# One-bank PSUM tiles and a five-block state scan in a decay-attention and mixer kernel

## The chip, the cores and the metric

The kernel runs on one core of a Trainium2 chip. The metric is the device time of one execution in microseconds (us). The engines are named as in the profile: PE (TensorE, matrix products; PEld are its weight loads), DVE (VectorE), ACT (ScalarE), POOL (GpSimd) and SP (SyncE, which issues DMAs). Each engine works off its own instructions in the order written; semaphores tie the engines together. SBUF is the working memory; PSUM, in banks of 512 fp32 columns on 128 partitions, takes the results of PE.

## What is computed

Decay attention over four batches and eight heads (768 positions, head width 64, blocks of 64 positions), and behind it a mixer with two products over the positions and two over the channels. Cut to what matters:

```python
# attention, for each batch b and head h; lam[h] is the decay
for b in range(nb):                         # nb = 12 blocks of 64
    intra = einsum('bhic,bhjc->bhij', qb, kb) * Dmask     # lam ** (i - j), i >= j
    intra = einsum('bhij,bhjd->bhid', intra, vb)
    inter = einsum('bhid,bhde->bhie', qb * lam_pow, kv_state)
    out[block b] = intra + inter
    kv_state = lam ** 64 * kv_state + einsum('bhsd,bhse->bhde', kb * rev_pow, vb)
# mixer, on x = out as (4, 768, 512)
u = x + (maximum(x.T @ w_tok1, 0) @ w_tok2).T
return u + maximum(u @ w_ch1, 0) @ w_ch2
```

## The kernel before

Two heads at a time form a pair; there are 16 pairs (4 batches, 4 pairs each). A chunk is 128 positions, two blocks `y` = 0 and 1 on partitions 0 to 63 and 64 to 127; a pair has `NC` = 6 chunks. The order of all engines is the order of the source (`manual_schedule`), so a loop written by hand (L717) sets who stands behind whom.

In pass `i` of this loop, with `j = i - 1`, PE does in turn: `scores(i+1)`, whose results DVE multiplies by the mask in `weigh`; `state(i+1)`; `carry(i, False)`; `carry(j, True)`; `outputs(j)`; the transposes of `turn_k(i+2)` and, for the first eight pairs, `turn_q_rows`; then groups of work of the token mixing (`token_hidden`, `token_out`), between which `turn_back(j, 0)` and `turn_back(j, 1)` stand. Calls of `later` put pieces of the weights' conversion (L455 to L470, L623, L651) on ACT, DVE and POOL in between.

`state` (L298) makes for each chunk the two sums over its blocks, `kv[0]` and `kv[1]`, each in a bank of its own (`k0`, `k1`), 44 matmuls of 64 by 64 a pair (L309). A chunk's sum of both blocks is made in SBUF, in `both`: ACT scales `kv[0]` by the decay of a block (L314), DVE adds `kv[1]` (L315). `both` has six places per state element, the first of them zero, so that the scan L317 over `D` × 6 elements begins each row of states anew (`keep` holds the decay, and zero at each first place). L325 makes the states of the odd blocks. POOL then copies the half of the states that is needed on the other partitions to `st` (L333, `place`), since `carry` (L381) multiplies heads crosswise.

`xTs[i]` collects the transposed output of a pair. It is one tile of two banks, `[P, 2, 512]` (L371), half `y` for the blocks `y`; tags `x0` and `x1` alternate by pair. `carry` and `outputs` (L397) add into it, and ACT copies it to `uT` after chunk 2 and after chunk 5 (L407), each time three chunks of both halves. `turn_back(j, x)` (L414) transposes three chunks back into half `x` of the same tile (L426), and ACT and DVE split the result into `xhi` (L432) and `xlo` (L433). The last group of work of a pass may borrow half 0 (`parting`, L760; `group_bank`, L526); other groups take that one of the banks `s0`, `s1`, `k0`, `k1` which was taken longest ago (`lease`).

Behind attention, two tiles of two banks each give the four entries of `spread` (L811). `bank("sh", ...)` (L115) takes entries 0, 1, 2 in turn, `bank("xT", ...)` entry 3. The products of the mixer's second layer go there: `mm2` (L1112), added to `uT` by L1125, and later `half` (L1167), added by L1182 and L1184. The first layer (`product`, L911) uses `s0` to `k1`.

```python
L371  xTs[i] = ps.tile([P, 2, CB], F32, tag=f"x{i % 2}", bufs=1, name=f"xT{i}")
L760  parting.append(xTs[j][:, 0])
L812  t = ps.tile([P, 2, CB], F32, tag=f"x{x}", bufs=1, name=f"spread{x}")
L813  spread.extend((t[:, 0], t[:, 1]))
```

Of the kernel before, what the change touches and what calls it, by code (L numbers as in the profile page):

```python
# [25 lines left out]
def kernel(  # L26
# [23 lines left out]
    nc = tc.nc  # L50
# [58 lines left out]
    turn_of = {}  # L109
    spread = []  # L110

# [3 lines left out]
    def bank(tag, nm, n):  # L115
        x = turn_of[tag] = turn_of.get(tag, -1) + 1
        if tag == "sc":
            return psum(("s0", "s1", "k0", "k1")[x % 4], nm, n)
        return spread[3 if tag == "xT" else x % 3][:, :n]

# [82 lines left out]

    keep = ap.tile([P, NP, D, NC], F32, name="keep")
    diag = ap.tile([P, D], F32, name="diag")
# [21 lines left out]
    def rows_of(x):  # L227
        return slice(x * D, (x + 1) * D)

    both = ap.tile([P, D, NC], F32, name="both")  # L230
    nc.gpsimd.memset(both, 0.0)
    nc.gpsimd.memset(keep, 0.0)
# [14 lines left out]
    for p in range(NP):  # L247
        nc.gpsimd.tensor_copy(out=keep[:, p, :, 1:], in_=fall2[:, p : p + 1, None].broadcast_to([P, D, NC - 1]))

# [48 lines left out]
    def state(i):  # L298

        b, p = pairs[i]  # L300
        kv = [lease(f"kv{i}{y}", S // 2, f"k{y}").rearrange("p (c e) -> p e c", e=D) for y in range(2)]
        for c in range(NC):
            x, m = spot(i, c)
            for y in range(2):
                if 2 * c + y == 2 * NC - 1:
                    continue
                r = rows_of(y)
                for h in range(2):
                    nc.tensor.matmul(  # L309
                        out=kv[y][rows_of(h), :, c], lhsT=kds[i][r, h, m, x], rhs=vns[i][r, h, c], start=True, stop=True  # L310
                    )
        by = fall[:, p : p + 1]
        n = NC - 1
        nc.scalar.mul(both[:, :, 1:], kv[0][:, :, :n], by)  # L314
        nc.vector.tensor_add(out=both[:, :, 1:], in0=both[:, :, 1:], in1=kv[1][:, :, :n])  # L315
        sv = ap.tile([P, 2, D, NC], F32, tag="sv", bufs=2, name=f"sv{i}")
        nc.vector.tensor_tensor_scan(  # L317
            out=sv[:, 0].rearrange("p e c -> p (e c)"),
            data0=keep[:, p].rearrange("p e c -> p (e c)"),
            data1=both.rearrange("p e c -> p (e c)"),  # L320
            initial=0.0,
            op0=ALU.mult,
            op1=ALU.add,
        )
        nc.vector.scalar_tensor_tensor(  # L325
            out=sv[:, 1], in0=sv[:, 0], scalar=by, in1=kv[0], op0=ALU.mult, op1=ALU.add
        )
        st = ap.tile([P, 2, 3, D], F32, tag="st", bufs=2, name=f"st{i}")
        states[i] = sv, st

        def place():
            for h in range(2):
                nc.gpsimd.tensor_copy(  # L333
                    out=st[rows_of(1 - h)], in_=sv[rows_of(h), :, :, chunks(i, 1 - h)].rearrange("p y e c -> p y c e")
                )

        return place
# [30 lines left out]
    def carry(i, same):  # L368

        if not same:  # L370
            xTs[i] = ps.tile([P, 2, CB], F32, tag=f"x{i % 2}", bufs=1, name=f"xT{i}")  # L371
        sv, st = states[i]
        for m in range(3):
            for x in range(2):
# [5 lines left out]
                for h in range(2):  # L380
                    nc.tensor.matmul(  # L381
                        out=xTs[i][rows_of(h), y, c * D : (c + 1) * D],
                        lhsT=sv[r, y, :, c] if h == x else st[r, y, m],
                        rhs=qss[i][r, h, m, y * D : (y + 1) * D],
                        start=not same and m == 0,
                        stop=False,
                        skip_group_check=True,
                    )

    def outputs(i):  # L390
        b, p = pairs[i]
        for c in range(NC):
            x, m = spot(i, c)
            for y in range(2):
                r = rows_of(y)
                for h in range(2):
                    nc.tensor.matmul(  # L397
                        out=xTs[i][rows_of(h), y, c * D : (c + 1) * D],
                        lhsT=vns[i][r, h, c],
                        rhs=weights_of[i, x][r, h, m],  # L400
                        start=False,
                        stop=(c % 3 == 2),
                        skip_group_check=True,
                    )
            if c % 3 == 2:
                cs = slice(c - 2, c + 1)
                nc.scalar.copy(  # L407
                    out=uT[b][:, p].rearrange("p (c y s) -> p c y s", y=2, s=D)[:, cs],
                    in_=xTs[i][:, :, : S // 2].rearrange("p y (c s) -> p c y s", s=D)[:, cs],
                )  # L410

    x_of = {}

    def turn_back(i, x):  # L414
# [7 lines left out]
        xhi, xlo = x_of[b, half]  # L422
        xp = xTs[i][:, x, : 3 * P]
        cs = slice(3 * x, 3 * x + 3)
# [101 lines left out]
    def group_bank(nm, n):  # L526
        if spread:
            return bank("sh", nm, n)
# [188 lines left out]
    for i in range(-2, NI + 1):  # L717
# [39 lines left out]
        for n in range(3):  # L757
            for f in work[cuts[n] : cuts[n + 1]]:
                if f is work[-1] and n == 2 and len(work) > 1:
                    parting.append(xTs[j][:, 0])  # L760
                f()
# [48 lines left out]
    later(99)  # L810
    for x in range(2):  # L811
        t = ps.tile([P, 2, CB], F32, tag=f"x{x}", bufs=1, name=f"spread{x}")  # L812
        spread.extend((t[:, 0], t[:, 1]))  # L813
    att.close()
# [757 lines left out]
```

## Time and profile before

| | |
|---|---|
| median of 3 runs | 647.53 us |
| lowest and highest | 644.53 and 647.7 us |
| the profiled execution | 649.42 us |
| its span, first to last instruction | 647.6 us |
| busy in the span: PE, DVE, ACT, POOL | 556.8, 403.7, 259.4, 295.9 us |
| mean granted clock of PE | 0.962 |

The span is what the profile shows; 1.8 us lie around it. Busy time is the time in which an engine had an instruction of its own under way, and PE's includes matmuls that overlap. The granted clock is a share of PE's full speed. A wait is named by the instruction that waited and the instruction whose end released it.

### The profile page before, as it was taken

The numbers are of one execution on the slowest core, as the hardware profiler recorded it, in microseconds if no ns is written. First come the engines' busy times: TensorE is split into PE (matmuls) and PEld (weight loads), VectorE is DVE, ScalarE is ACT, GpSimd is POOL, SyncE is SP. The second block draws the span as 40 slices with busy tenths as digits, with TensorE's granted clock in tenths as the row PEclk, the third lists the DMA queues.
The fourth block names the chain that finished last, engine by engine and source line by source line (L and its number), as shares of the span: only waits on it lengthen the run. The fifth ranks groups of instructions, "written<-read, shape, count | busy, mean of one in ns | idle before, by whom it ended". The sixth has DMA issues, their size and how long they took to land.

```text
span 647.6 us, 12886 instructions
## 1 busy us (share of the span) xinstructions
PE 556.8 (86%) x5246; PEld 466.0 (72%) x5246; DVE 403.7 (62%) x589; ACT 259.4 (40%) x471; POOL 295.9 (46%) x257
## 2 busy tenths in 40 slices
PE   5646777867788777989889999999898899999997
PEld 4546776757677676867678778887677678878885
DVE  4446746666657436656777957667946766556555
ACT  3445543354432323445445453434345523323211
POOL 5634543755332504365465685246467721315000
PEclk9987988999989968989999999999999999999999
DMA  9986085466741001657486567895824578656106
GB/s 192 221 201 148 10 175 134 94 151 165 197 96 59 2 1 67 233 222 284 155 303 245 221 254 181 216 333 182 310 74 149 179 174 216 260 211 211 33 1 130
DMA packets 162954, 108.32 MB, mean 167 GB/s; under 512 B 132560, under 2 KB 147408, under 8 KB 162896
## 3 DMA queue, kind: packets, MB, share of 16 engines
q1 hardware_dynamic: 153168, 86.92, 48.6%
q10 hardware_dynamic: 9728, 20.58, 8.5%
q8 instruction: 41, 0.67, 0.4%
q14 instruction: 17, 0.14, 0.1%
HBM read 75.50 MB, written 31.98 MB: 166 GB/s over the span
## 4 chain that ended last, share of the span: by engine, by line
PE 70%; DVE 11%; ACT 8%; DMA 4%; issue 4%; POOL 2%; SPq 0%; ACTq 0%; DVEq 0%; POOLq 0%
PE spread L1167 14%; PE b L911 13%; PE spread L1112 11%; PE d L911 6%; PE a L911 3%; PE xT L381 3%; PE xT L547 3%; DMA raw<-in_moe_w_ch_dram 2%; PE xT L397 2%; PE pu L568 2%; PE ph L547 2%; PE kv L309 2%; PE sc L348 2%; DVE xlo L433 2%; PE xT L426 1%
## 5 line engine op out<-in xcount | busy, mean ns | idle before, releaser
L292 POOL TENSOR_TENSOR qs<-qT,lamp 128x384 f32<-128x384 f32 x32 | 39.2, 1246 | 74.8 <-PE xT L381 74.8
L1125 DVE TENSOR_TENSOR uT<-spread,uT 128x512 f32<-128x512 f32 x63 | 43.3, 687 | 24.8 <-PE spread L1112 24.3
L1112 PE MATMUL spread<-hh,c2h 128*128 128x512 f32 x96 | 39.0, 407 | 9.7 <-DVE uT L1125 9.7
L1112 PE MATMUL spread<-hh,c2l 128*128 128x512 f32 x96 | 38.3, 399 | 0.0
L1112 PE MATMUL spread<-hl,c2h 128*128 128x512 f32 x96 | 38.1, 397 | 0.0
L1182 DVE TENSOR_TENSOR uT<-spread,uT 128x512 f32<-128x512 f32 x50 | 32.8, 684 | 6.2 <-PE spread L1167 6.2
L433 DVE TENSOR_TENSOR xlo<-xT,xhi 128x384 fp32r<-128x384 f32 x32 | 17.8, 556 | 27.9 <-ACT xhi L432 27.5
L397 PE MATMUL xT<-a,vn 64*64 64x64 f32 x720 | 23.2, 232 | 12.8 <-ACT uT L407 8.5
L426 PE MATMUL xT<-ident,uT 128*128 128x128 f32 x96 | 17.9, 300 | 17.9 <-DVE xlo L433 16.7
L333 POOL COPY st<-sv 64x384 f32<-64x384 f32 x32 | 29.0, 907 | 9.4 <-DVE sv L325 8.0
L1112 PEld LDWEIGHTS spread<-hh,c2h 128*128 128x128 f32 x96 | 18.2, 189 | 17.4 <-DVE uT L1125 13.5
L932 POOL TENSOR_TENSOR hl1x<-t,hh1x 128x512 fp32r<-128x512 f32 x8 | 10.6, 1326 | 42.9 <-ACT hh1x L926 42.9
L407 ACT COPY uT<-xT 128x384 f32<-128x384 f32 x32 | 15.3, 479 | 36.9 <-PE xT L397 36.9
L397 PEld LDWEIGHTS xT<-a,vn 64*64 64x64 f32 x720 | 18.9, 138 | 15.2 <-ACT uT L407 10.6
L381 PE MATMUL xT<-qs,sv 64*64 64x64 f32 x352 | 26.2, 284 | 1.1 <-DVE hl L552 1.0
L426 PEld LDWEIGHTS xT<-ident,uT 128*128 128x128 f32 x96 | 12.2, 152 | 20.5 <-DVE xlo L433 18.6
L317 DVE TENSOR_TENSOR_SCAN sv<-keep,both 128x384 f32<-128x384 f32 x16 | 24.0, 1499 | 4.5 <-PE xT L381 3.8
L911 PE MATMUL b<-o,c1h 128*128 128x512 f32 x72 | 26.2, 404 | 0.0
L911 PE MATMUL a<-o,c1h 128*128 128x512 f32 x72 | 25.4, 393 | 0.0
L932 POOL TENSOR_TENSOR tt<-t,tt 128x512 fp32r<-128x512 f32 x12 | 17.0, 1421 | 16.8 <-ACT tt L926 16.8
L381 PEld LDWEIGHTS xT<-qs,sv 64*64 64x64 f32 x352 | 23.7, 205 | 1.4 <-POOL o L684 1.2
L432 ACT CAST xhi<-xT 128x384 fp32r<-128x384 f32 x32 | 15.4, 480 | 22.4 <-PE xT L426 22.4
(423 smaller groups left out, 1842.7 us busy)
## 6 DMA issues: line engine op xcount, KB each, us to landing
c1h<-k SPq DMA_DIRECT2D x12, 896.0 KB, 5.4
c1l<-k SPq DMA_DIRECT2D x12, 896.0 KB, 7.9
raw<-in_moe_w_ch_dram SPq DMA_DIRECT2D x7, 1024.0 KB, 6.6
vn<-in_v_dram SPq DMA_DIRECT2D x15, 384.0 KB, 5.0
k<-c1h ACTq DMA_DIRECT2D x6, 896.0 KB, 4.9
k<-c1l ACTq DMA_DIRECT2D x6, 896.0 KB, 4.0
out_dram<-y SPq DMA_DIRECT2D x72, 64.0 KB, 2.5
c2lx<-k SPq DMA_DIRECT2D x7, 512.0 KB, 4.5
```

Of the source, the lines that this page charges most:

```text
L292: nc.gpsimd.tensor_mul(out=qss[i][:, h].rearrange("p m (y i) -> p (m y) i", i=D), in0=qTs[i].rearrange("p (h n i) -> p h n i", h=2, i=D)[: ...
L333: nc.gpsimd.tensor_copy(out=st[rows_of(1 - h)], in_=sv[rows_of(h), :, :, chunks(i, 1 - h)].rearrange("p y e c -> p y c e"))
L381: nc.tensor.matmul(out=xTs[i][rows_of(h), y, c * D : (c + 1) * D], lhsT=sv[r, y, :, c] if h == x else st[r, y, m], rhs=qss[i][r, h, m, y * ...
L397: nc.tensor.matmul(out=xTs[i][rows_of(h), y, c * D : (c + 1) * D], lhsT=vns[i][r, h, c], rhs=weights_of[i, x][r, h, m], start=False, stop= ...
L426: nc.tensor.transpose(out=xp[:, m * P : (m + 1) * P], in_=uT[b][:, p, c * P : (c + 1) * P], identity=ident)
L433: nc.vector.tensor_sub(out=lo, in0=src, in1=hi.bitcast(F32))
L547: nc.tensor.matmul(out=ph, lhsT=w[:, c, fs], rhs=x[:, c], start=(i == 0), stop=(i == 3 * NC - 1))
L911: nc.tensor.matmul(out=c[into], lhsT=w[:, WI[o], ct], rhs=x[:, ct], start=(first and i == 0), stop=(i == 5), skip_group_check=True,)
L1112: nc.tensor.matmul(out=po, lhsT=w[:, jj, cs], rhs=h, start=(i == 0), stop=(i == 3 * JG - 1), skip_group_check=n >= NG)
L1125: nc.vector.tensor_add(out=ub, in0=two(po), in1=ub)
L1167: nc.tensor.matmul(out=G[into, t], lhsT=w2[:, v, j, t * P : (t + 1) * P], rhs=x, start=(o in (5, 1, 2) and not second and i == 0), stop=(i ...
L1182: nc.vector.tensor_add(out=ub, in0=two(G[into, t]), in1=ub)
```

## The change

Every PSUM tile becomes one bank. `xTs[i]` is a list of two tiles, tags `x00`, `x01`, `x10` and `x11`; `bank` hands out these four tags in the same turn as the entries of `spread`, each time as a new tile. `outputs` copies to `uT` only after chunk 5, once for each bank. `kv[0]` and `kv[1]` are laid out with the chunk innermost, six and five places per state element, so that a matmul writes with a step of 6 or 5 elements. ACT scales `kv[0]` into `half_kv` in SBUF, DVE adds it onto `kv[1]` in PSUM, and the scan reads that sum, over `D` × 5 elements. The first block state, which was the scan's sixth place, is copied from `kv[0]` by two small ACT copies, to `s1` and to `st`; `carry` reads `s1` and `sv[..., c - 1]`, and `place` copies one column less for the even half.

```diff
     def bank(tag, nm, n):
         x = turn_of[tag] = turn_of.get(tag, -1) + 1
         if tag == "sc":
             return psum(("s0", "s1", "k0", "k1")[x % 4], nm, n)
-        return spread[3 if tag == "xT" else x % 3][:, :n]
+        return psum("x11" if tag == "xT" else ("x00", "x01", "x10")[x % 3], nm, n)
...
-    keep = ap.tile([P, NP, D, NC], F32, name="keep")
+    keep = ap.tile([P, NP, D, NC - 1], F32, name="keep")
...
-    both = ap.tile([P, D, NC], F32, name="both")
-    nc.gpsimd.memset(both, 0.0)
+    half_kv = ap.tile([P, D, NC - 1], F32, name="half_kv")
...
-        kv = [lease(f"kv{i}{y}", S // 2, f"k{y}").rearrange("p (c e) -> p e c", e=D) for y in range(2)]
+        kv = [lease(f"kv{i}{y}", D * n, f"k{y}").rearrange("p (e c) -> p e c", c=n) for y, n in enumerate((NC, NC - 1))]
...
-        n = NC - 1
-        nc.scalar.mul(both[:, :, 1:], kv[0][:, :, :n], by)
-        nc.vector.tensor_add(out=both[:, :, 1:], in0=both[:, :, 1:], in1=kv[1][:, :, :n])
-        sv = ap.tile([P, 2, D, NC], F32, tag="sv", bufs=2, name=f"sv{i}")
+        sv = ap.tile([P, 2, D, NC - 1], F32, tag="sv", bufs=2, name=f"sv{i}")
+        st = ap.tile([P, 2, 3, D], F32, tag="st", bufs=2, name=f"st{i}")
+        s1 = ap.tile([P, D], F32, tag="s1", bufs=2, name=f"s1{i}")
+        states[i] = sv, st, s1
+        nc.scalar.mul(half_kv, kv[0][:, :, : NC - 1], by)
+        for h in range(2):
+            nc.scalar.copy(out=(st[rows_of(0), 1, 0] if h else s1[rows_of(0)]), in_=kv[0][rows_of(h), :, 0])
+        nc.vector.tensor_add(out=kv[1], in0=half_kv, in1=kv[1])
         nc.vector.tensor_tensor_scan(
             out=sv[:, 0].rearrange("p e c -> p (e c)"),
             data0=keep[:, p].rearrange("p e c -> p (e c)"),
-            data1=both.rearrange("p e c -> p (e c)"),
+            data1=kv[1].rearrange("p e c -> p (e c)"),
...
         nc.vector.scalar_tensor_tensor(
-            out=sv[:, 1], in0=sv[:, 0], scalar=by, in1=kv[0], op0=ALU.mult, op1=ALU.add
+            out=sv[:, 1], in0=sv[:, 0], scalar=by, in1=kv[0][:, :, 1:], op0=ALU.mult, op1=ALU.add
         )
...
         def place():
             for h in range(2):
+                x = 1 - h
+                cs = range(NC)[chunks(i, x)][1 - x :]
                 nc.gpsimd.tensor_copy(
-                    out=st[rows_of(1 - h)], in_=sv[rows_of(h), :, :, chunks(i, 1 - h)].rearrange("p y e c -> p y c e")
+                    out=st[rows_of(x), :, 1 - x :],
+                    in_=sv[rows_of(h), :, :, cs[0] - 1 : cs[-1] : cs[1] - cs[0]].rearrange("p y e c -> p y c e"),
                 )
...
-            xTs[i] = ps.tile([P, 2, CB], F32, tag=f"x{i % 2}", bufs=1, name=f"xT{i}")
-        sv, st = states[i]
+            xTs[i] = [psum(f"x{i % 2}{y}", f"xT{i}{y}", CB) for y in range(2)]
+        sv, st, s1 = states[i]
...
-                        lhsT=sv[r, y, :, c] if h == x else st[r, y, m],
+                        lhsT=st[r, y, m] if h != x else sv[r, y, :, c - 1] if c else s1[r],
...
-                        stop=(c % 3 == 2),
+                        stop=(c == NC - 1),
                         skip_group_check=True,
                     )
-            if c % 3 == 2:
-                cs = slice(c - 2, c + 1)
-                nc.scalar.copy(
-                    out=uT[b][:, p].rearrange("p (c y s) -> p c y s", y=2, s=D)[:, cs],
-                    in_=xTs[i][:, :, : S // 2].rearrange("p y (c s) -> p c y s", s=D)[:, cs],
-                )
+        for y in range(2):
+            nc.scalar.copy(
+                out=uT[b][:, p].rearrange("p (c y s) -> p y c s", y=2, s=D)[:, y],
+                in_=xTs[i][y][:, : S // 2].rearrange("p (c s) -> p c s", s=D),
+            )
...
-                    parting.append(xTs[j][:, 0])
+                    parting.append(xTs[j][0])
...
-    for x in range(2):
-        t = ps.tile([P, 2, CB], F32, tag=f"x{x}", bufs=1, name=f"spread{x}")
-        spread.extend((t[:, 0], t[:, 1]))
+    mixing = True
```

## Rows read from the trace of the kernel before

**Rows 1.** Busy times by stretches: us, each engine's busy us (instructions), clock, DMA.

```profile
0.00:240.00 240.00, 174.95 (x3585) 157.22 (x3586) 134.23 (x213) 98.62 (x195) 110.07 (x115) 0.92 0.55 125
...
sum 648.00, PE 556.76 PEld 466.04 DVE 403.70 ACT 259.42 POOL 295.92; mean PE 139.19 PEld 116.51 DVE 100.92 ACT 64.86 POOL 73.98
```

**Rows 2.** Tile `xT`, instructions of PE: idle until (us, times).

```profile
  DVE xlo L433: 34.7, 17
  ACT uT L407: 10.3, 18
```

**Rows 3.** Tile `spread`, instructions of PE: idle until (us, times).

```profile
  DVE uT L1125: 9.7, 8
  DVE uT L1184: 5.5, 3
  DVE uT L573: 3.6, 2
  DVE hl L552: 1.8, 1
```

**Rows 4.** Timeline at 121 us: start, us, instruction, [idle before <-releaser].

```profile
121.53 0.56 DVE L433 TENSOR_TENSOR xlo<-xT,xhi 128x384 fp32r<-128x384 f32 x1 [0.28 <-ACT xhi L432]
122.14 0.39 PE L547 MATMUL xT<-xhi,w1h 128*128 128x256 f32 x1 [1.16 <-DVE xlo L433]
```

**Rows 5.** Timeline at 327 us, in the mixer.

```profile
327.20 0.67 DVE L1125 TENSOR_TENSOR uT<-spread,uT 128x512 f32<-128x512 f32 x1
...
327.93 0.50 PE L1112 MATMUL spread<-hh,c2h 128*128 128x512 f32 x1 [1.63 <-DVE uT L1125]
```

**Rows 6.** Timeline at 61 to 65 us, in pass 2.

```profile
61.48 0.90 PE L426 MATMUL xT<-ident,uT 128*128 128x128 f32 x3 [3.51 <-DVE xlo L433]
62.15 0.69 DVE L462 SCALAR_TENSOR_TENSOR uT<-uT 128x512 uint32<-128x512 uint32 x1
...
64.73 0.36 PE L381 MATMUL xT<-qs,st 64*64 64x64 f32 x1
```

**Rows 7.** The page's costliest groups: busy us, mean ns | idle before, releaser.

```profile
L407 ACT COPY uT<-xT 128x384 f32<-128x384 f32 x32 | 15.3, 479 | 36.9 <-PE xT L397 36.9
```

**Rows 8.** Line 317 by itself: ns min/median/max, first and last start.

```profile
L317 DVE TENSOR_TENSOR_SCAN sv<-keep,both x16: 957/1724/1798, 13.1 to 212.2; 128x384 f32<-128x384 f32 x16
```

**Rows 9.** Timelines at 13 and at 54 us, DVE and POOL.

```profile
13.13 0.96 DVE L317 TENSOR_TENSOR_SCAN sv<-keep,both 128x384 f32<-128x384 f32 x1
...
54.24 2.60 POOL L292 TENSOR_TENSOR qs<-qT,lamp 128x384 f32<-128x384 f32 x2 [4.56 <-PE xT L381]
54.25 1.79 DVE L317 TENSOR_TENSOR_SCAN sv<-keep,both 128x384 f32<-128x384 f32 x1 [0.27 <-PE xT L381]
```

**Rows 10.** Line 325 by itself, and who waited for it (us, times).

```profile
L325 DVE SCALAR_TENSOR_TENSOR sv<-sv,fall,kv x16: 612/615/616, 14.2 to 214.0; 128x384 f32<-128x384 f32 x16
...
  PE pu L568: 1.9, 3
  PE ph L547: 1.7, 2
```

**Rows 11.** Line 951, an add whose output `d` is in PSUM: ns min/median/max.

```profile
L951 DVE TENSOR_TENSOR d<-d,u x6: 687/690/700, 269.6 to 383.0; 128x512 f32<-128x512 f32 x6
```

**Rows 12.** Weight loads of line 381: ns min/median/max.

```profile
L381 PEld LDWEIGHTS xT<-qs,sv x352: 183/206/223, 19.1 to 232.8; 64*64 64x64 f32 x176
L381 PEld LDWEIGHTS xT<-qs,st x352: 129/133/228, 19.2 to 232.8; 64*64 64x64 f32 x176
```

**Rows 13.** Stretches from one `state` to `carry`, and from `carry` to `outputs`.

```profile
183.44:184.04 0.60, 0.60 (x56) 0.60 (x49) 0.60 (x2) 0.00 (x0) 0.00 (x0) 1.00 0.00 0
184.04:185.07 1.03, 1.03 (x56) 1.03 (x49) 1.03 (x2) 0.53 (x1) 0.00 (x0) 1.00 0.08 16
```

**Rows 14.** Stretches of 18 matmuls of L547 after a wait, and of 20 without.

```profile
178.85:182.69 3.84, 3.84 (x18) 3.71 (x18) 0.55 (x1) 0.00 (x0) 0.00 (x0) 0.56 0.67 108
173.27:175.43 2.16, 2.16 (x20) 2.16 (x20) 0.73 (x2) 2.15 (x4) 2.04 (x3) 1.00 1.13 342
```

More of the change, by code (lines that the diff above doesn't have):

```diff
@@ L109 @@
     turn_of = {}
-    spread = []
+    mixing = False
     def psum(tag, nm, n):
@@ L247 @@
     for p in range(NP):
-        nc.gpsimd.tensor_copy(out=keep[:, p, :, 1:], in_=fall2[:, p : p + 1, None].broadcast_to([P, D, NC - 1]))
+        nc.gpsimd.tensor_copy(out=keep[:, p, :, 1:], in_=fall2[:, p : p + 1, None].broadcast_to([P, D, NC - 2]))
     kTs, qTs, qss, kds, weights_of, scored = {}, {}, {}, {}, {}, {}
@@ L325, in state @@
         nc.vector.scalar_tensor_tensor(
-            out=sv[:, 1], in0=sv[:, 0], scalar=by, in1=kv[0], op0=ALU.mult, op1=ALU.add
+            out=sv[:, 1], in0=sv[:, 0], scalar=by, in1=kv[0][:, :, 1:], op0=ALU.mult, op1=ALU.add
         )
-        st = ap.tile([P, 2, 3, D], F32, tag="st", bufs=2, name=f"st{i}")
-        states[i] = sv, st
         def place():
             for h in range(2):
+                x = 1 - h
+                cs = range(NC)[chunks(i, x)][1 - x :]
                 nc.gpsimd.tensor_copy(
-                    out=st[rows_of(1 - h)], in_=sv[rows_of(h), :, :, chunks(i, 1 - h)].rearrange("p y e c -> p y c e")
+                    out=st[rows_of(x), :, 1 - x :],
+                    in_=sv[rows_of(h), :, :, cs[0] - 1 : cs[-1] : cs[1] - cs[0]].rearrange("p y e c -> p y c e"),
                 )
@@ L381, in carry @@
                     nc.tensor.matmul(
-                        out=xTs[i][rows_of(h), y, c * D : (c + 1) * D],
-                        lhsT=sv[r, y, :, c] if h == x else st[r, y, m],
+                        out=xTs[i][y][rows_of(h), c * D : (c + 1) * D],
+                        lhsT=st[r, y, m] if h != x else sv[r, y, :, c - 1] if c else s1[r],
                         rhs=qss[i][r, h, m, y * D : (y + 1) * D],
@@ L397, in outputs @@
                     nc.tensor.matmul(
-                        out=xTs[i][rows_of(h), y, c * D : (c + 1) * D],
+                        out=xTs[i][y][rows_of(h), c * D : (c + 1) * D],
                         lhsT=vns[i][r, h, c],
@@ L422, in turn_back @@
         xhi, xlo = x_of[b, half]
-        xp = xTs[i][:, x, : 3 * P]
+        xp = xTs[i][x][:, : 3 * P]
         cs = slice(3 * x, 3 * x + 3)
@@ L526, in group_bank @@
     def group_bank(nm, n):
-        if spread:
+        if mixing:
             return bank("sh", nm, n)
```

## The prediction

> **What bounds the kernel now.** I read first the table of busy times by stretches: TensorE (PE) is busy for 556.8 of 647.6 us, DVE for 403.7, the other engines for less than half. Up to 240 us (attention, with the token mixing woven in) PE is busy for 175.0 of 240 us, at a granted clock of 0.92 [rows 1]. So time can be won where PE stands still. Then I ask for PE's instructions that write the two-bank tiles and what ended PE's idle time before them: for `xT` 34.7 us in 17 waits for L433 and 10.3 us for L407 [rows 2], for `spread` 9.7, 5.5, 3.6 and 1.8 us [rows 3]. That is 65.6 of the 90.8 us in which PE is idle.
>
> Whether these waits are needed is read from the timeline. At 122.14 the first matmul of the group of work that borrows `xTs[j][:, 0]` (`parting`, L760) starts 1.16 us late, behind the L433 of 121.53 [rows 4]. That L433 belongs to `turn_back(j, 1)` and reads the other half. In the mixer the matmul at 327.93 starts 1.63 us late, behind the L1125 of 327.20, which adds the product made just before [rows 5]; yet the halves are taken in turn, and its own was last used three products earlier. So the wait is for the neighbour in the tile. The waits for L407 are another kind: `outputs` writes both halves while the first copy reads from both.
>
> **Part 1, one bank per tile.** The bare chain from the last L426 over one L432 and one L433 is the 1.16 us at 122.14. What is longer is a queue. Pair 1 is an example: PE waits 3.51 us at 61.48, since ACT has three operations of a weight conversion in front of L432. After the change PE goes on at once, but DVE still has L459 and L462 ahead of the second L433. I walk it with this order: L462 ends at 62.15 + 0.69 = 62.84 [rows 6], L433 takes 0.56 [rows 4], so at 63.4 the tile is free that `carry(i+1)` writes. `carry` started at 64.73 [rows 6]; 1.3 of the 3.5 us come through. So of each of the 17 waits I count 1.16 us and nothing of the excess: 19.7 us. Next late is `carry` on L433, behind the conversions. A bare wait comes through whole, because `scores` and `state` (0.6 us and more each) stand between `turn_back` and `carry`.
>
> The copies of `outputs` move behind all 24 + 24 matmuls, one for each bank. 16 waits of 0.57 us go (9.1 of the 10.3 us); in exchange both copies (479 ns each, [rows 7]) now follow the last matmul, and the transposes of `turn_back(j, 0)` need both, because `uT` is ordered by chunks. Where `turn_k`'s six transposes stand between, some 0.2 us are left over; in the last two pairs nothing stands between. I count 14 × 0.4 = 5.6 us.
>
> Behind attention 14 waits, 20.6 us [rows 3]. After the change each bank waits only for its own reader, three products back, which in the cases I looked at was done. But DVE stays as late as it was, and up to 310 us it is late because the conversions wait for loads. I keep two thirds, 13.7 us. This share is a choice; ends 6 and 20.6.
>
> **Part 2, the scan.** L317 takes 957 ns at least and 1724 at the median [rows 8]. At 13.13 it ran alone in 0.96 us; at 54.25 it started with POOL's first L292 and took 1.79 [rows 9]. L325, whose second input is in PSUM, lies in part under the same POOL pair and keeps to 612 to 616 ns in all 16 [rows 10]. So the length comes from two inputs in SBUF beside POOL, and a scan that reads `kv[1]` from PSUM should lose it. For five blocks in place of six I take 957 × 5/6 = 0.80 us, and 0.51 for L325: 0.7 to 0.9 us less a pair where POOL was beside it. This counts where PE waits for L325, which frees the bank of the next group: 3.6 us in five waits [rows 10]. PE comes there up to 0.57 us earlier by part 1, so I count 2.5 us. The add L315 now writes PSUM: adds that do so take 690 ns for 512 columns [rows 11], L433 writes SBUF in 0.56 us for 384 [rows 4], about in proportion, so no cost.
>
> **Part 3, what is added.** Two ACT copies of 64 columns a pair, each between 0.08 (a sixth of L407's 479 ns, for a sixth of its columns) and 0.48 us. They stand between L314 and the first L407; ACT is idle there for 36.9 us in 32 cases, waiting for `outputs` [rows 7], and that hides them. Without this cover they would cost 2.5 to 15 us. L325, two DVE operations later, is the only other one behind them. POOL's second L333 shrinks by a third; POOL is not on the path. `carry` still loads `sv` with a step.
>
> The doubtful edit: L309's 704 matmuls (44 a pair) now write with a step of 6 or 5 elements, where every output of before is contiguous. No row shows such a write. Lower end zero: 44 of them take 0.60 us (183.44 to 184.04, [rows 13]), on four quadrants 55 ns for 64 columns each, 0.85 ns a column, and a slower write can hide behind that. A gain has no reason. The nearest rows are loads with a step: L381's weight load takes 206 ns from `sv` (a step of 6) and 133 from `st` (contiguous) [rows 12], and `carry`'s 44 matmuls, 22 of them with such a load, need 1.03 us [rows 13]: (1.03 − 0.60) / 22 = 20 ns of PE time each. Upper end by this: 704 × 20 = 14 us. I take zero, because a stepped load stands in front of its matmul while a write drains behind it, and keep 14 us for the range.
>
> The Trainium skill speaks against this edit: its page "PSUM — Partial Sum Buffer", section Specifications (TRN2), states lines of 8 bytes and that any non-contiguous access pattern slows matmuls significantly. It gives no figure, and no run of before shows it on an output. By that rule the time would lie at 618 or beyond, where the sum by rows says 604.
>
> **The clock.** From 178.85, behind a wait of 3.1 us, 18 matmuls took 3.84 us at a granted clock of 0.56, near the lower level (1.2 GHz); as many and two more took 2.16 us at 1.00, the level of 2.4 GHz [rows 14]. Such a stretch costs 1.7 us. The long waits become shorter, not nothing, so I count one and a bit: 2 us; ends 0 and 12.
>
> **Sum.** 19.7 + 5.6 + 13.7 + 2.5 + 2 = 43.5 us. The profiled execution took 649.42 us (its span 647.6 and 1.8 around it), 0.3% above the median of 647.53; the same 43.5 us off the median give **604 us**.
>
> **The rivals.**
> - *Everything comes through:* 34.7 + 8 + 20.6 + 3.6 + 6 of clock = 73, so 575 us. Against it: the walk at 61.48. Chance 0.06.
> - *The order on ACT and DVE takes the place of the banks:* conversions stay in front of L432, L433 and L1125, and PE meets the same lateness one step later. Half of 43.5 is kept: 626 us. For it: DVE is busy for 62% of the span [rows 1] and stands in strict order. Against it: the 1.16 us have no queue in them. Chance 0.17.
> - *The step of the output costs 20 ns a matmul:* 604 + 14 = 618 us. Chance 0.10. This is the page's rule at its mild end.
> - *The change doesn't do what it says:* the semaphores still tie neighbours together, and only copy and scan gain, 8 us: 640 us. Against it: rows 4 and 5. Chance 0.05.
> - *Slower:* each matmul of L309 pays the whole 73 ns (206 − 133) of the load's row, and the quadrants don't overlap it: 704 × 73 = 51 us, so 655. It decides from 66 ns a matmul on, (43.5 + 3.2) / 704. The page's rule would be its reason. Against it: the 20 ns of `carry`. Chance 0.06.
>
> **How the numbers follow.** The forecast has 0.56 and reaches from 590 to 618. Low 586 cuts off the first rival; high 632 takes in the stepped one and most of the queue, and leaves out the last two: about 0.82 inside. This kernel can be told from no change by about 0.5%, 3.2 us. Faster by more 0.90, within 0.04 (parts of the fourth rival and of the tails), slower 0.06.
>
> **What would show it.** Right: before instructions that write the `x` banks PE's idle time for L433 and L407 falls from 45 to under 10 us, behind attention from 20.6 to under 7; a new wait of `carry`, on L433 or on the readers of the borrowed bank, has some 10 us; all 16 scans take 0.8 to 0.9 us; 44 matmuls of L309 still take 0.6 us. Wrong: L309 needs over 1 us; the scan from PSUM takes over 1.2 us; `turn_back(j, 0)` waits for L407 in every pair; or the mixer is no shorter, and DVE's lateness was paid at another place.

## The result and the profile after

The changed kernel takes 583.05 us (median; 581.66 to 583.34) where the kernel before, timed beside it, takes 647.62 us: a ratio of 0.9005, 95% interval 0.8971 to 0.904. The gain is 64.6 us; the forecast was 43.5 us, and 583 lies below the range that began at 586.

Where the time went is read from the table of busy times by stretches. I cut both runs at the same places of the program: the first matmul of `product` (L911 before, L912 after), which comes 18 times in groups of 42; the same after 6 and after 12 of these groups; and the end. The columns are those of [rows 1]. First the kernel before, then the one after:

```profile
0.00:237.80 237.80, 172.75 (x3581) 155.44 (x3581) 132.91 (x210) 98.14 (x194) 110.07 (x115) 0.93 0.56 126
237.80:386.10 148.30, 133.18 (x578) 107.81 (x577) 103.89 (x135) 67.81 (x112) 84.91 (x67) 0.97 0.56 210
386.10:507.45 121.35, 117.45 (x499) 94.09 (x498) 81.99 (x116) 52.16 (x93) 68.86 (x52) 0.99 0.66 205
507.45:647.60 140.15, 133.38 (x593) 108.69 (x591) 84.91 (x130) 41.31 (x73) 32.09 (x24) 1.00 0.55 160
```

```profile
0.00:199.03 199.03, 161.59 (x3580) 147.71 (x3581) 118.75 (x209) 100.18 (x226) 98.09 (x114) 0.96 0.67 150
199.03:325.69 126.66, 126.04 (x579) 104.81 (x578) 101.82 (x136) 67.58 (x113) 84.61 (x66) 1.00 0.65 242
325.69:440.41 114.72, 114.28 (x500) 93.42 (x498) 81.26 (x114) 50.95 (x91) 68.68 (x53) 1.00 0.71 221
440.41:579.87 139.46, 133.25 (x593) 108.68 (x591) 86.75 (x132) 42.57 (x76) 34.13 (x25) 0.99 0.56 161
```

The first stretch, attention with the token mixing in it, is 38.8 us shorter, the second 21.6, the third 6.6, the last 0.7. PE does the same matmuls in each (give or take one at a border), so its time splits in two: idle time and busy time.

| stage | idle before, after | idle less | busy before, after | busy less |
|---|---|---|---|---|
| attention (row 1) | 65.1, 37.4 us | 27.6 us | 172.8, 161.6 us | 11.2 us |
| behind it (rows 2 to 4) | 25.8, 7.3 us | 18.5 us | 384.0, 373.6 us | 10.4 us |

So 46.1 us are waits that went, which the forecast had at 41.5, and 21.6 us are the same matmuls done in less time. The granted clock is 0.96 in place of 0.93 in the first stretch and 1.00 in place of 0.97 in the second. The forecast had 2 us for the clock. The two sums make 67.7 us, the distance of the two profiled executions; the medians lie 64.6 apart.

What stops PE now, in the list of PE's waits of the kernel after (us in total, times, longest us):

```profile
PE xT L385 <- DVE xlo L436: 5.5, 4, 3.0
...
PE kv L308 <- DMA vn<-in_v_dram: 4.1, 2, 3.7
PE kv L308 <- POOL kd L283: 4.0, 6, 1.8
PE qt L273 <- DVE sv L328: 3.8, 4, 1.8
...
PE xT L429 <- ACT uT L410: 1.7, 2, 0.9
PE pu L571 <- DVE sv L328: 1.5, 1, 1.5
...
PE kt L258 <- DVE sv L320: 1.3, 1, 1.3
...
PE ph L550 <- DVE sv L328: 1.0, 1, 1.0
```

The counterpart of [rows 2], what ended PE's idle time before it writes an `x` bank, is now:

```profile
  DVE xlo L436: 6.7, 5
  ACT uT L410: 1.7, 2
  DVE uT L576: 1.3, 1
  DVE hl L555: 0.8, 1
```

The 45.0 us for L433 and L407 have become 8.4 us for L436 and L410, the same two instructions. Of the waits for L1125 in [rows 3] nothing is left. The page's row of the matmuls that begin a product of the mixer's second layer, before and after (the last figures are the idle time in front of them):

```profile
L1112 PE MATMUL spread<-hh,c2h 128*128 128x512 f32 x96 | 39.0, 407 | 9.7 <-DVE uT L1125 9.7
```

```profile
L1113 PE MATMUL po<-hh,c2h 128*128 128x512 f32 x96 | 37.6, 392 | 0.0
```

A place like that of [rows 5] shows how. In this timeline of after, DVE is late by the same conversion as before (L465 until 271.34) and adds the product of 268.06 to 269.59 (ended long before) only at 271.86. PE has not waited for that: at 270.79 it began the next product of this layer in the next bank, and its matmuls start 0.23 us one behind the other:

```profile
269.63 1.71 DVE L465 SCALAR_TENSOR_TENSOR wa<-wa,t 128x1024 uint32<-128x1024 uint32 x1
...
270.79 0.39 PE L1113 MATMUL po<-hh,c2h 128*128 128x512 f32 x1
...
271.69 0.39 PE L1113 MATMUL po<-hh,c2l 128*128 128x512 f32 x1
...
271.86 0.68 DVE L1126 TENSOR_TENSOR uT<-po,uT 128x512 f32<-128x512 f32 x1
271.92 0.39 PE L1113 MATMUL po<-hl,c2h 128*128 128x512 f32 x1
...
272.14 0.39 PE L912 MATMUL d<-o7h,c1h 128*128 128x512 f32 x1
```

The single instructions, as ns min/median/max: the scan from PSUM (L320), L328 and POOL's `qs` (L291), which answer to [rows 8 to 10], and the outer products with their stepped output (L308):

```profile
L320 DVE TENSOR_TENSOR_SCAN sv<-keep,kv x16: 819/821/822, 12.2 to 181.9; 128x320 f32<-128x320 f32 x16
L328 DVE SCALAR_TENSOR_TENSOR sv<-sv,fall,kv x16: 546/547/549, 13.2 to 182.9; 128x320 f32<-128x320 f32 x16
L291 POOL TENSOR_TENSOR qs<-qT,lamp x32: 984/998/1007, 9.7 to 182.9; 128x384 f32<-128x384 f32 x32
L308 PE MATMUL kv<-vn,kd x660: 212/218/363, 9.6 to 180.3; 64*64 64x64 f32 x165
```

### The profile page after: what moved, and what is told of

It reads as the page before. It is cut to its first block, busy times and chain, and to the rows that moved or that the text cites. A ratio compares the mean times of both kernels' runs of the same rounds, so it can differ in the third digit from the quotient of the medians.

```text
span 579.9 us, 12903 instructions
## 1 busy us (share of the span) xinstructions
PE 535.2 (92%) x5246; PEld 454.6 (78%) x5246; DVE 388.6 (67%) x589; ACT 261.3 (45%) x503; POOL 285.5 (49%) x256
## 4 chain that ended last, share of the span: by engine, by line
PE 70%; DVE 12%; ACT 7%; DMA 5%; issue 3%; POOL 2%; DVEq 0%; ACTq 0%; POOLq 0%
PE b L912 14%; PE gb L1168 9%; PE po L1113 8%; PE d L912 7%; PE gc L1168 6%; PE pu L571 4%; PE a L912 4%; PE ph L550 3%; PE xT L385 3%; DMA raw<-in_moe_w_ch_dram 3%; PE gb L1113 2%; PE xT L401 2%; PE gc L1113 2%; DVE sv L320 1%; DMA vn<-in_v_dram 1%
## 5 line engine op out<-in xcount | busy, mean ns | idle before, releaser
L291 POOL TENSOR_TENSOR qs<-qT,lamp 128x384 f32<-128x384 f32 x32 | 31.3, 999 | 66.0 <-PE xT L385 59.2
L1126 DVE TENSOR_TENSOR uT<-po,uT 128x512 f32<-128x512 f32 x48 | 32.8, 683 | 10.4 <-PE po L1113 9.8
L1113 PE MATMUL po<-hh,c2l 128*128 128x512 f32 x96 | 37.7, 393 | 0.0
L1113 PE MATMUL po<-hl,c2h 128*128 128x512 f32 x96 | 37.6, 392 | 0.0
L1113 PE MATMUL po<-hh,c2h 128*128 128x512 f32 x96 | 37.6, 392 | 0.0
L436 DVE TENSOR_TENSOR xlo<-xT,xhi 128x384 fp32r<-128x384 f32 x32 | 17.6, 554 | 23.9 <-ACT xhi L435 23.6
L933 POOL TENSOR_TENSOR hl1x<-t,hh1x 128x512 fp32r<-128x512 f32 x8 | 10.6, 1325 | 41.8 <-ACT hh1x L927 41.8
L336 POOL COPY st<-sv 64x384 f32<-64x384 f32 (+1 forms) x32 | 25.5, 797 | 7.4 <-DVE sv L328 6.1
L1183 DVE TENSOR_TENSOR uT<-gb,uT 128x512 f32<-128x512 f32 x40 | 26.1, 682 | 3.9 <-PE gb L1168 3.9
L912 PE MATMUL a<-o,c1h 128*128 128x512 f32 x72 | 25.5, 394 | 1.5 <-DVE hh0x L923 1.1
L912 PE MATMUL b<-o,c1h 128*128 128x512 f32 x72 | 25.3, 392 | 0.0
L308 PE MATMUL kv<-vn,kd 64*64 64x64 f32 x660 | 14.9, 225 | 9.5 <-DMA vn<-in_v_dram 4.1
L316 ACT ACTIVATE half_kv<-kv,fall 128x320 f32<-128x320 f32 x16 | 8.4, 527 | 29.5 <-PE kv L308 29.5
L401 PE MATMUL xT<-a,vn 64*64 64x64 f32 x720 | 21.2, 237 | 0.5 <-issue 0.5
L258 PE MATMUL kt<-ident,kn 128*128 128x128 f32 x90 | 15.9, 320 | 6.2 <-DMA kn<-in_k_dram 4.8
L571 PE MATMUL pu<-w2h,hh 128*128 128x384 f32 x56 | 20.0, 357 | 1.6 <-DVE sv L328 1.5
L308 PEld LDWEIGHTS kv<-vn,kd 64*64 64x64 f32 x660 | 13.0, 139 | 10.6 <-issue 6.6
L629 POOL TENSOR_TENSOR c1l<-wa,c1h 128x512 fp32r<-128x512 f32 (+1 forms) x12 | 15.3, 1292 | 12.2 <-ACT c1h L626 12.1
L1113 PEld LDWEIGHTS po<-hh,c2h 128*128 128x128 f32 x96 | 18.0, 188 | 4.0
## 6 DMA issues: line engine op xcount, KB each, us to landing
vn<-in_v_dram SPq DMA_DIRECT2D x15, 384.0 KB, 5.8
```

The lines of the kernel that those rows point to most:

```text
L291: nc.gpsimd.tensor_mul(out=qss[i][:, h].rearrange("p m (y i) -> p (m y) i", i=D), in0=qTs[i].rearrange("p (h n i) -> p h n i", h=2, i=D)[: ...
L308: nc.tensor.matmul(out=kv[y][rows_of(h), :, c], lhsT=kds[i][r, h, m, x], rhs=vns[i][r, h, c], start=True, stop=True)
L336: nc.gpsimd.tensor_copy(out=st[rows_of(x), :, 1 - x :], in_=sv[rows_of(h), :, :, cs[0] - 1 : cs[-1] : cs[1] - cs[0]].rearrange("p y e c -> ...
L401: nc.tensor.matmul(out=xTs[i][y][rows_of(h), c * D : (c + 1) * D], lhsT=vns[i][r, h, c], rhs=weights_of[i, x][r, h, m], start=False, stop= ...
L571: nc.tensor.matmul(out=pu, lhsT=h[:, kk, cs], rhs=w[:, kk, ss], start=(i == 0), stop=(i == 3 * NK - 1))
L912: nc.tensor.matmul(out=c[into], lhsT=w[:, WI[o], ct], rhs=x[:, ct], start=(first and i == 0), stop=(i == 5), skip_group_check=True,)
```

## The experiments

### The two halves of the change: banks alone, scan alone

The diffs of this chapter are cut; `...` marks what is left out. `e1_banks_only` is the changed kernel with the state's part as it was before; `e2_scan_only` is the changed kernel with the two-bank tiles, `spread` and the two copies of `outputs` as they were before.

```diff
 e1_banks_only, against the kernel after
-        nc.vector.tensor_add(out=kv[1], in0=half_kv, in1=kv[1])
+        nc.vector.tensor_add(out=both[:, :, 1:], in0=both[:, :, 1:], in1=kv[1][:, :, :n])
...
-            data1=kv[1].rearrange("p e c -> p (e c)"),
+            data1=both.rearrange("p e c -> p (e c)"),
...
 e2_scan_only, against the kernel after
-            xTs[i] = [psum(f"x{i % 2}{y}", f"xT{i}{y}", CB) for y in range(2)]
+            xTs[i] = ps.tile([P, 2, CB], F32, tag=f"x{i % 2}", bufs=1, name=f"xT{i}")
...
```

> The one-bank tiles, with the copies of outputs behind all its matmuls, but the states' scan as in the kernel before (six blocks, sum in SBUF, matmuls of L309 with contiguous output). My theory (the scan only shortens the wait of PE for the bank that L325 frees, some 2.5 us): 586 us. Rival A (the scan carries a large part of the change, since POOL's pair of multiplications is also freed from it, 31.3 against 39.2 us): 595 us or more. Rival B (the stepped output of L309 costs something that the contiguous one gives back): under 583 us.

> The kernel before with only the states' part changed: sum in PSUM, stepped output of L309, scan over five blocks; two-bank tiles as before. Theory: 643 to 645 us, because only the waits of PE for L325 (3.6 us) go and the waits for the neighbour bank stay. Rival A: 635 us or less. Rival B (the stepped output costs PE time): 648 us or more, with over 1 us for 44 matmuls of L309 in place of 0.6 us.

Measured: 589.54 us for the banks alone (ratio 0.9117, 0.9049 to 0.9185) and 642.59 us for the scan alone (0.993, 0.9897 to 0.9964). The kernel before took 648.74 us beside them. So the banks bring 57 us by the ratio and 59 by the medians, the scan 4.5 us (2.3 to 6.7) by itself by the ratio and 6.2 by the medians, and 6.5 us (589.54 − 583.05, two groups of runs) on top of the banks. Whether the scan is worth more with the banks than alone, these numbers do not tell. `e1_banks_only` ends between its theory (586) and rival A (595 or more); rival B, under 583, falls, and so does that of `e2_scan_only` in which the step costs time (648 or more). With the banks PE does wait more for the tiles that DVE frees behind the scan. The list of PE's waits of `e1_banks_only` shows them:

```profile
PE pu L567 <- DVE sv L325: 4.4, 3, 2.0
PE ph L546 <- DVE sv L325: 3.5, 3, 2.1
PE qt L274 <- DVE sv L325: 2.2, 1, 2.2
```

10.1 us for L325, where before it was 3.6 us in five waits [rows 10]; with the scan in PSUM 6.3 us are left for L328. What makes the scan shorter is read from its rows in the two kernels, first with two SBUF inputs, then with one from PSUM:

```profile
L317 DVE TENSOR_TENSOR_SCAN sv<-keep,both x16: 957/1580/1805, 12.7 to 188.6; 128x384 f32<-128x384 f32 x16
```

```profile
L320 DVE TENSOR_TENSOR_SCAN sv<-keep,kv x16: 820/821/821, 12.3 to 209.1; 128x320 f32<-128x320 f32 x16
```

With the input in PSUM all sixteen take the same time, also where POOL's `qs` runs beside them: in the kernel after, the scan of 54.64 us takes 0.82 us while L291 runs from 54.36 to 56.31. Five blocks in place of six can account for a sixth of the time (0.96 to 0.80 us), not for the spread up to 1.8 us that went; no run has a scan of five blocks from SBUF.

### Where the banks count: behind attention, and in attention

`e3_mixer_banks` is the kernel before, and only behind attention the four entries of `spread` become tiles of one bank. `e4_attn_banks` is the kernel after, and only behind attention there are tiles of two banks again.

```diff
 e3_mixer_banks, against the kernel before
-        return spread[3 if tag == "xT" else x % 3][:, :n]
+        t = "x11" if tag == "xT" else ("x00", "x01", "x10")[x % 3]
+        return spread[0].tile([P, n], F32, tag=t, bufs=1, name=nm)
...
 e4_attn_banks, against the kernel after
-        return psum("x11" if tag == "xT" else ("x00", "x01", "x10")[x % 3], nm, n)
+        return spread[3 if tag == "xT" else x % 3][:, :n]
...
```

Both also take these tiles from a pool of their own, which is closed behind attention and opened anew.

> The kernel before with one-bank tiles only behind attention; attention as before. Theory (every wait for the neighbour bank there is pure loss, and the lower clock that follows long waits goes with it): the stretch from the first product of the mixer to the end shortens as in the changed kernel, by 29 us, so 618 to 621 us, and PE's idle time there falls from 20.6 to under 3 us. Rival C (my forecast: DVE's lateness comes back as another wait, two thirds kept, clock 2 us): 632 us. Rival D (the stretch is shorter in the changed kernel only because attention ends earlier and the weights' loads lie differently): 640 us or more.

> The changed kernel with one-bank tiles in attention only; behind it the two tiles of two banks of the kernel before. Theory (the two parts are independent): attention as in the changed kernel, 583 + 29 = 612 us. Rival D: 595 us or less.

Measured: 619.21 us (0.9557, 0.9482 to 0.9632) and 609.43 us (0.9412, 0.9358 to 0.9466), beside 648.74 us for the kernel before. The 29.5 us and 39.3 us (28.7 and 38.1 by the ratios) add up to 68.8, near the whole: the two stages don't trade with each other. 619.21 lies within the 618 to 621 us of its theory and 609.43 near the 612 of the other; the rivals C (632) and D (640 or more; 595 or less) fall. The stretches of each run, attention and the rest:

```profile
0.00:232.10 232.10, 167.66 (x3580) 150.07 (x3581) 132.38 (x210) 97.97 (x194) 110.12 (x115) 0.93 0.57 129
232.10:612.38 380.28, 373.31 (x1669) 307.07 (x1667) 269.57 (x379) 160.73 (x277) 187.01 (x142) 1.00 0.63 206
```

```profile
0.00:198.33 198.33, 161.50 (x3580) 148.10 (x3581) 118.83 (x209) 99.86 (x226) 98.21 (x114) 0.95 0.68 151
198.33:607.72 409.39, 382.30 (x1669) 309.33 (x1667) 270.94 (x380) 161.67 (x278) 186.13 (x142) 0.99 0.59 192
```

Behind attention one bank per tile takes 409 us down to 380, whatever attention does. The pool is not the reason: `e4_attn_banks` opens it anew too, and with tiles of two banks it needs 409.4 us where the kernel before needs 409.8. The busy time of the same 1669 matmuls falls from 382.3 to 373.3 with it. Attention of unchanged code is 237.8 us in one profile of the kernel before and 232.1 us in `e3_mixer_banks`, so of a single profile a few us of attention mean nothing; the timed ratios carry the sum.

### The copies alone

`e5_copy_only` is the kernel before with the copies to `uT` behind all matmuls of `outputs`, one for each half.

```diff
-                        stop=(c % 3 == 2),
+                        stop=(c == NC - 1),
...
-            if c % 3 == 2:
...
+        for y in range(2):
+            nc.scalar.copy(
+                out=uT[b][:, p].rearrange("p (c y s) -> p y c s", y=2, s=D)[:, y],
+                in_=xTs[i][:, y, : S // 2].rearrange("p (c s) -> p c s", s=D),
+            )
```

> The kernel before with only the copies of outputs moved behind its last matmul, one for each half; the tiles stay two banks. Forecast: 5.6 us less than before (0.9%), PE's waits in outputs for L407 gone, and in the last two pairs turn_back waits for the copies as it did. Rival: the time goes to the waits for the neighbour bank, which end at the same moment, and the kernel is the same within 0.3%.

Measured: 645.13 us, a ratio of 0.9945 (0.9903 to 0.9986), about 3.5 us, with an interval from 0.9 to 6.3 that barely leaves out no change and holds the forecast of 5.6. What PE stood idle for before it writes `xT`:

```profile
  DVE xlo L432: 34.4, 17
...
  ACT uT L406: 2.1, 3
```

The 16 waits of 0.57 us are gone as forecast (10.3 us for the copy in [rows 2], 2.1 here), but some of it comes back: in PE's list of waits L325 stands with 8.7 us in place of 3.6, and ACT's copy of `kT`, before the transposes of `q`, with 4.0 in place of 1.5. PE is earlier, DVE and ACT are not.

### What a wait costs: short and long waits made on purpose

The mixer gained 29 us, and its waits before were 20.6 us [rows 3]. To see whether a wait costs more than it lasts, both of these kernels add to the kernel after, at the head of five groups of products of the first layer (12 to 16, counted from 0, where PE hardly waits), a transpose into the product's bank, copies on POOL that need it, and a second transpose that needs them. They differ in the number of POOL's copies: two in `e6_stall_short`, whose diff stands here, and eight in `e7_stall_long`. The products' results are the same.

```diff
+        if s == 0 and 12 <= n <= 16:
+            nc.tensor.transpose(out=c[into][:, :P], in_=ident, identity=ident)
+            for _ in range(2):
+                nc.gpsimd.tensor_copy(out=ident, in_=ident)
+            nc.tensor.transpose(out=c[into][:, :P], in_=ident, identity=ident)
```

> The changed kernel with a made wait in front of product 0 of the groups 12 to 16 of the mixer, where PE is busy without a break at a granted clock of 1.00: a transpose, two copies of the identity matrix onto itself on POOL, a transpose that waits for them (both overwritten by the product). Control for the long one: 5 waits of some 1 us and 10 transposes, so 6 us more than the changed kernel (589 us), and no stretch at the lower clock behind them.

> The same with eight copies on POOL, so 5 waits of some 3 us. Theory (a long wait costs itself and then some 1.7 us at the lower clock): 5 x (3 + 0.5 + 1.7), 25 us more than the changed kernel, and a stretch with granted clock 0.5 behind each wait. Rival (a wait costs only itself; the clock in the kernel before has another cause): 17 us more, clock 1.00 behind them.

Measured: 593.17 us (0.9157, 0.9108 to 0.9206) and 612.38 us (0.9461, 0.939 to 0.9531), that is 10 us and 29 us above the kernel after (583.05, in another group of runs). The made waits in the two lists of PE's waits:

```profile
PE b L913 <- POOL ident L912: 9.9, 5, 6.5
```

```profile
PE b L913 <- POOL ident L912: 20.5, 5, 8.7
```

The short kernel's waits, 9.9 us in all, cost about what they last, with ten transposes; the long one's, 20.5 us, cost 29. In both the first wait is longer than was meant (6.5 and 8.7 us, behind other work on POOL), so the short kernel lies 4 us above its forecast of 589. The two kernels differ by 10.6 us of made waits and by 19.2 us of time, so the rival, a wait that costs only itself, falls. That the mixer before also had 20.6 us of waits and lost 29 is in part chance: it had 14 waits, here there are five. One group shows what happens (group 13, from its first own matmul to that of the next, with one made wait in it); the kernel after, the short wait of 0.84 us, the long one of 2.97 us:

```profile
461.84:481.05 19.21, 19.21 (x86) 15.77 (x84) 14.14 (x23) 5.97 (x11) 4.03 (x3) 1.00 0.90 219
```

```profile
468.35:488.89 20.54, 19.70 (x87) 15.90 (x88) 14.20 (x24) 6.42 (x12) 4.96 (x5) 1.00 0.87 214
```

```profile
473.82:497.91 24.09, 21.12 (x88) 17.00 (x88) 13.30 (x21) 6.34 (x11) 6.65 (x12) 0.93 0.89 246
```

With the wait of 0.84 us the clock stays at 1.00 and the group costs 1.33 us more, the wait and 0.49 us of busy time for two transposes. With the wait of 2.97 us, 2.13 us longer, the group takes 3.55 us longer: PE is 1.42 us longer busy with the same work, at a granted clock of 0.93. Right behind such a wait the granted clock is 0.50, the level of 1.2 GHz:

```profile
473.82:476.60 2.78, 2.78 (x8) 2.20 (x9) 0.58 (x1) 0.00 (x0) 1.05 (x1) 0.50 0.99 285
```

There the timeline of `e7_stall_long` has matmuls of 0.63 and 0.77 us,

```profile
473.69 0.47 PE L913 MATMUL b<-ident 128*128 128x128 f32 x1 [2.97 <-POOL ident L912]
473.82 0.77 PE L917 MATMUL b<-o,c1h 128*128 128x512 f32 x1
474.39 0.63 PE L917 MATMUL b<-o,c1l 128*128 128x512 f32 x1
```

where matmuls of this shape take 0.39 us elsewhere, as in the timeline at 272.14 above. Against the same groups of `e6_stall_short`, PE is busy 1.3 to 1.4 us longer behind three of the four waits of 2.97 us and 2.8 us behind the last one (granted clock 0.86). So in this kernel a wait of about 3 us costs about half as much again behind it, or more. The one long wait of `e6_stall_short` (6.5 us) is of the same kind: the granted clock of the group behind it was 0.92.

### Two waits that are left, and a faster kernel

The list of after names two waits in attention whose cause is an order of issue. `carry` waits for L436, the end of the second `turn_back`; where a pass has no group of work between its two, that one still stands behind pieces of the weights' conversion (`e8_turns_first` puts both together there). And L308 waits for POOL's `kd` because the scaling of the keys stands behind `place` on POOL (`e9_kd_first` issues it ahead). `e10_both` has both; the kernel after is timed beside the last two.

```diff
 e8_turns_first
-            if n < 2 and j >= 0:
+            if n < 2 and j >= 0 and (n == 0 or cuts[1] < cuts[2]):
                 turn_back(j, n)
+                if n == 0 and cuts[1] == cuts[2]:
+                    turn_back(j, 1)
 e9_kd_first
+        if i >= 1 and i + 2 < NI:
+            scale_k(i + 2)
         if place:
             place()
-        if 1 <= i < NP:
-            scale_k(i + 2)
...
-            if n == 0 and i + 2 < NI and not 1 <= i < NP:
+            if n == 0 and i + 2 < NI and i < 1:
                 scale_k(i + 2)
```

> The changed kernel; where no group of work stands between turn_back(j, 0) and turn_back(j, 1), the second now comes straight after the first, ahead of the pieces of the weights' conversion on ACT and DVE. Theory (what is left of the long waits is the order on ACT and DVE, as in my walk): the waits of carry for L436 (5.5 us in four) go, and the kernel is 3 to 6 us faster. Rival (the conversions come later by as much and their readers wait): same within 0.3%.

> The changed kernel as it is, timed beside the next two on the same chip. Expected 583 us (581.5 to 584.5) and a ratio to the kernel before of 0.897 to 0.903; the two kernels beside it are to be read against this one.

> The changed kernel with the scaling of the keys (L283 on POOL, its other half on ACT) issued ahead of the state's placement (L336) from pair 1 on, in place of behind it; nothing else moves. Theory: the 4.0 us (6 waits) that the first matmuls of the outer products (L308) spend waiting for kd are there because L283 stands behind two placements of 0.8 us on POOL's queue. Ahead of them those waits fall below 1.5 us, and the kernel is 2 to 4 us faster than the changed one (579 to 581). Rival: the placement, now 0.83 us later, makes the carried products (L385) wait for L336 by as much as was gained; then the time is the changed one's within 1 us. Second rival, slower by 1 to 3 us: ACT's half of the scaling, issued earlier, stands ahead of the copies out of the outputs (L410), and the transposes of L429 wait more than the 1.7 us of now.

> The kernel of e9_kd_first with the edit of e8_turns_first on top: where an iteration has no conversion between its two turn_backs, both sets of transposes stand together, and DVE's work behind them is issued earlier. Theory: the two edits take away different waits (that for kd, and that of the carried products for L436), so their gains add: that of e8 was about 2.5 us, that of e9 2 to 4 us, together 4 to 6.5 us under the changed kernel (576.5 to 579). Rival: both waits are in series behind the same DVE or POOL work, and the second gives nothing beyond the first (within 1 us of e9_kd_first).

Measured: `e8_turns_first` 580.52 us (0.8957, 0.8906 to 0.9007; 2.5 us below the 583.05 of after, timed in another group of runs, so not certain; the waits of `carry` for L436, which were to go, fell from 5.5 to 4.0 us). In one group: after 582.67 us (580.87 to 584.15), `e9_kd_first` 577.09 us (576.18 to 577.95), `e10_both` 574.59 us (572.64 to 576.43). So the edit of `e9_kd_first` brings 5.6 us and that of `e8_turns_first` 2.5 us more on top, where their runs overlap a little; the two gains add, as the theory of `e10_both` said, to more than its 4 to 6.5 us. The kernel with both stands at 0.8891 (0.8841 to 0.8941) of the kernel before and 8.1 us below the changed one, with no overlap of their runs.

`e9_kd_first` gained more than the 2 to 4 us forecast, and its waits say why. In PE's list of the kernel after, from this group of runs:

```profile
PE xT L385 <- DVE xlo L436: 6.9, 4, 3.1
PE kv L308 <- DMA vn<-in_v_dram: 6.2, 3, 3.9
PE kv L308 <- POOL kd L283: 4.0, 6, 1.8
```

and in `e9_kd_first`:

```profile
PE xT L385 <- DVE xlo L436: 10.7, 4, 3.6
PE kv L308 <- POOL kd L283: 0.8, 2, 0.5
```

The wait for `kd` fell as forecast. The wait for `vn`, a load, went with it, which was not forecast. Its cause is read from the list of waits of SP's queue, first in the kernel after, then in `e9_kd_first`:

```profile
SPq L179 <- ACT kd L285: 19.3, 6, 7.3
```

```profile
SPq L179 <- ACT kd L285: 10.0, 8, 2.1
```

SP stood in front of a load of keys (L179), up to 7.3 us at a time, until ACT's half of the scaling had read the old ones, and the load of `vn` (L193) stood behind it. With the scaling earlier the longest such wait is 2.1 us, and SP comes to the load of `vn` ahead of time: there it now waits for PE to free the buffer (for L401, 26.6 us in nine waits, before 7.7 us in one). No run moves the load alone, so this part is read from the lists and not tested. Against it `carry` waits 3.8 us more for L436: the rival had the place right and the instruction wrong (not L336).

## Why the prediction was wrong, step by step

**The clock: the step that failed.** The sum had 2 us for it, with 12 as its upper end; by the granted clock of the two profiled executions it gave up to 14.7 us, and the same matmuls took 21.6 us less in all. The forecast took one stretch at 1.7 us [rows 14], near the 1.42 us of `e7_stall_long`, and counted it "one and a bit" times, as if hardly any wait but the longest had such a tail, and as if the long waits would become shorter only. Every made wait of about 3 us had one, and the 17 waits for L433 had a mean of 2.0 us (34.7 / 17, [rows 2]); where between 0.84 and 2.97 us the tail begins, no run shows. The size could have been read from the column that stands in [rows 1]: at 0.92 over 240 us, and at a mean of 0.962 over the span, the lower clock takes up to (1 − 0.962) × 647.6 = 24.6 us; after it is (1 − 0.983) × 579.9 = 9.9. "Up to", because this counts time in which PE was idle too.

**What the sum left out beside it.** The other 7 of the 21.6 us the forecast put at nothing. A wait also breaks up the overlap of matmuls. In the timeline at 271 us they start 0.23 us apart though each lasts 0.39; the last one before a wait overlaps with nothing and counts 0.16 us more as busy, and the first one behind it lasts 0.50 us in [rows 5], 0.11 more. For the 14 waits that went behind attention this is an estimate of 14 × 0.27 = 3.8 us. The clock, by its two digits in the table, gives about (1 − 0.97) × 148.3 + (1 − 0.99) × 121.35 = 5.7 us there, so that 9.5 of the 10.4 us are accounted for. In attention the matmuls have other shapes and new waits took the place of some old ones, so there the split stays open; no run took it apart.

**Behind attention: two thirds was too little.** I kept 13.7 of the 20.6 us because DVE stays late. DVE is as late as before, and PE no longer meets it: it uses three banks in turn, and in the timeline at 271 us it is at work in the next bank while DVE still has the last one to add. The idle time fell by 18.5 us and the waits at L1113 to nothing; `e3_mixer_banks` shows 29 us for this stage alone, clock and all.

**Waits in attention: the sum was right by luck.** 19.7 + 5.6 + 2.5 = 27.8 us were forecast, and PE's idle time there fell by 27.6, since errors cancelled. Before the `x` banks it fell by more (45.0 to 8.4 us for L433 and L407, where "under 10" was wanted), and other waits took some back: for `sv` (L320 and L328) 7.6 us in place of 3.6, for `kd` 4.0 in place of 1.6 in the list of before, for `vn` 4.1 us. The new wait of `carry` on L433's successor is there (5.5 us); with those on L576 and L555, 1.3 and 0.8 us, `carry` waits 7.6 us where "some 10 us" were forecast. The walk at 61.48 that put nothing of the excess through was right in its mechanism, as the new wait shows; as a count for all 17 waits it was too careful. The copies gave 3.5 us alone (`e5_copy_only`, 0.9 to 6.3) where 5.6 were counted, which is within its interval. The two waits for L410 are those of the last two pairs, as said.

**The scan.** 821 ns in all 16 (0.8 to 0.9 forecast) and 547 ns for L328 (510 forecast). Counted at 2.5 us, it is worth 4.5 alone (2.3 to 6.7) and 6.5 with the banks. That POOL's `qs` gains too was not in the forecast: one took up to 1710 ns before, and now none takes over 1007.

**The stepped output costs nothing.** The matmuls of L308 have a median of 218 ns (660 of the 704 are in the record), and that of L309, without a step, is 218 in `e1_banks_only` too:

```profile
L309 PE MATMUL kv<-vn,kd x660: 218/218/366, 9.5 to 187.0; 64*64 64x64 f32 x165
```

The ends of matmuls are modelled in the profile, so their starts count for more: those of the last pair begin at 179.66 and `carry` at 180.26, 0.60 us later, as in [rows 13]. So zero was right, and both the rival of 14 us and the slower one of 51 us fall. The rule of the Trainium skill, "PSUM — Partial Sum Buffer", section Specifications (TRN2), that any non-contiguous access pattern slows matmuls significantly, is not borne out for these fp32 outputs of 64 columns with a step of 5 or 6 elements.

**The rivals.** The one with everything coming through (575 us, chance 0.06) was the nearest to 583, but by two errors that balance: its waits were too many (67 us against 46) and its clock too small (6 against 21.6). The order on ACT and DVE, at 626, had the higher chance because DVE is busy for 62% of the span; that share says nothing of whether its lateness reaches PE, which has two or three banks in hand. That the change doesn't do what it says is out by `xT` and L1113.

## What to carry to other kernels

Where a wait of some microseconds goes away in front of PE, look at the granted clock of that stage as well as at the wait: here 46 us of waits took 22 us of PE's busy time with them, and (1 − clock) × time before (24.6 us, of which up to 14.7 went) bounds what the clock can give back. A wait for the neighbour in a tile of two banks is found by comparing, in the timeline, the releaser's operand with the bank that is written; with one tile per bank DVE's lateness in the mixer cost PE nothing here, because PE had other banks in hand. After such a change read the next queue from the list of waits: putting the scaling, which frees a load's buffer, ahead of the placement, for which PE did not wait, gave another 5.6 us.

## What the runs showed of the hardware

- A wait of 2.97 us on PE cost 1.42 us more of busy time behind it, at a granted clock of 0.93 over the group and of 0.50 in its first 2.8 us; one of 0.84 us left the clock at 1.00.
- A scan with two inputs in SBUF took 957 ns alone and up to 1805 (`e1_banks_only`) beside POOL, whose multiplies took up to 1710 ns; with one input in PSUM the scan took 819 to 822 ns for five sixths of the elements, and a multiply of POOL at most 1007.
- A matmul's output with a step of 5 or 6 fp32 elements in PSUM took no longer than a contiguous one: 44 such matmuls needed 0.60 us in both.
